# Reordering the start of a fused attention and mixture-of-experts kernel: early row writes ahead of late loads, the first tile's scaling on VectorE

## The chip, the cores and the metric

The kernel runs on 1 core of one Trainium2 chip, in one launch. The metric is device time in microseconds, as the median of the runs shown. A run's profile gives one execution, with its span from the first to the last instruction.

## The reference

Inputs `q`, `k`, `v` have the shape (8, 8, 576, 64): 8 batches, 8 heads, 576 tokens, 64 dimensions. The result has 8 × 576 = 4608 rows of 512.

```python
kv = np.einsum('bhsd,bhse->bhde', k, v)
out = np.einsum('bhsd,bhde->bhse', q, kv)
rms = np.sqrt(np.mean(out * out, axis=-1, keepdims=True) + 1e-06)
x = out / rms * g_norm          # then reshaped to 4608 rows of 512
logits = x @ w_gate             # 8 experts
e_idx = np.argmax(logits, axis=1)
gate_w = softmax(logits)[row, e_idx]
eom = 1 / (1 + np.exp(-(x @ w_output_gate)))
for e in range(8):              # rows whose best expert is e
    h = np.maximum(x[mask] @ w1[e], 0)      # 512 -> 1024
    out[mask] = gate_w * eom[:, e] * (h @ w2[e])   # 1024 -> 512
```

So each row goes to one expert out of eight, and which one is known only once its attention row is there.

## The kernel before, in words

**Tiles.** The 4608 tokens are 36 tiles of 128. For each of the 8 batches the kernel forms the `kv` matrix (`kv_part`, five steps of TensorE: four quarters of 128 tokens and a remainder of 64), transposes it (`kvT_part`, L589), multiplies it by the gate weights (`m_part`, L598), and then `out_tile` (L628) makes rows and logits of a tile of 128 tokens in one set of products, evicts them (`evict`, L677: rows to `xrow`, squares, logits), and writes pairs of tiles to the DRAM tensor `xs` (`xwrite`, L1050).

**Routing.** `route` (L711) runs in groups of 9, 7, 10 and 10 tiles on VectorE: the scale 1/rms of each row and head, logits, the best expert, the row's rank among its expert's rows (matmuls into `rps`), and a table of the rows of each expert (one-hot matrices `la` of VectorE, ScalarE and GpSimd, matmuls into `tblps`, L991). The table becomes row numbers in `gidx`. The scales go to small DRAM tensors (`xr0`, `xr`, `xt`).

**The early part.** The first 16 tiles (`EARLY`) are made and routed in `early` (L1108). After them the first two tiles of rows of every expert are known (the runs 0 to 7, 256 rows each). From then on the dense work goes on run by run (`run`, L1414), 8 runs of 256 rows and 8 of the rest, and what is left of the attention part (batches 4 to 7, tiles 16 to 35) is a generator, `late` (L1225), of which the dense loop takes one step, `next(rest)`, after each of its eight blocks of products.

**The first tile.** Run 0 is expert 0. The rows of its first 128 places are gathered from `xs` by an indirect DMA of GpSimd (`gather_row`, L315, called at L1006), their scales from `xr0` (L1200), both queued on GpSimd; `scale_rows` (L303, called at L1208) multiplies rows by scales on GpSimd (`scale_heads`, L298, is the multiplication on any engine). The second tile's gathers stand behind that on GpSimd (L1013), and its multiplication is on VectorE (L1491). `stage` (L322) transposes a tile on TensorE (L334, into `tps`); for run 0 ScalarE copies the result, times `g_norm`, to `xw` in fp32 (L338), then to the high part of a two-part form (`hi`, L340), and VectorE makes the low part `lo` (L341). `mm1_part` (L351) forms the first products of run 0 straight from `xw` and the unsplit weights `wraw`, for four of the eight blocks of 128 columns, first tile before second. All other products take three matmuls of high and low parts (`mm1`, L365, and `mm2`, L403).

**What sets the order.** Every engine's order is the program's order in this stretch (a manual schedule): TensorE, ScalarE, VectorE, GpSimd and SyncE each take their instructions as they are written. SyncE issues nearly all loads and the `xs` writes in one queue. `loads` is the list of early loads; `early_extra` holds those of batch 4 (four key-value quarters of 512 KB, one remainder) with query load 8 put third (L515 and L516); `send` issues the next of them, or a part of the first weights; `late_loads` holds all later ones. `constants(n)` puts n matmuls of constants into TensorE's order. The writes of tiles 14 and 15 (`held_row`, L668) are held back until all 16 tiles are done (L1183).

**Around L1183 to L1208**, in order: the held rows and the last write of `xs`; the rest of `early_extra`; the first step of `late` (quarters 0 and 1 of batch 4); the routing of the second group, with pauses numbered by `at_pause`: at 1 the second step of `late` (tile 16), at 6 the gather of the first tile's scales, the second quarter of the first weights (behind a GpSimd mark, `issue_mark`), two late loads and the third step (quarters 2 and 3), at 8 the scaling. `first_tile` (L1218) puts five constant matmuls, the fourth step (the remainder), `stage(0, 0)` and two constant matmuls. After the first products `stage(0, 1)` and two more steps of `late` follow (tile 17, `kvT_part`; L1501 to L1503), then `run(0)`.

```python
def scale_heads(x, tl, eng, heads=slice(0, H)):
    v = x.rearrange("p (h d) -> p h d", d=D)[:, heads]
    f = tl[:, heads].unsqueeze(2).to_broadcast(list(v.shape))
    return eng.tensor_tensor(out=v, in0=v, in1=f, op=ALU.mult)
```

Of the kernel before, what the change touches and what calls it, by code (L numbers as in the profile page):

```python
# [155 lines left out]
def body(ctx: ExitStack, tc: tile.TileContext, kvm, rem, qT, w1, w2, kc, xs, xr0, xr, xt, tab, out):  # L156
# [165 lines left out]
    def stage(i, k, eng=None):  # L322
# [13 lines left out]
        if not i:  # L336
            xw[k] = take([P, 4, P], F32, "xw")
            nc.scalar.activation(xw[k], ps, AF.Copy, scale=gcol[:, 0:1])  # L338
# [3 lines left out]
                                       in1=hi.bitcast(F32), op0=ALU.mult, op1=ALU.subtract)  # L342

# [172 lines left out]
    early_extra[2:2] = q_loads(nq + 1)  # L516
    late_loads = []
    g = EARLY
    for b in range(FIRST_B, B + 1):
        parts = []  # L520
        if b < B:
            kv = kv_loads(b) if b > FIRST_B else []
            parts = [kv[0:2], kv[2:4], rt_loads(b) if b > FIRST_B else []]
        for x, part in enumerate(parts):
            late_loads += part
            if (b > FIRST_B or x != 1) and g < tiles_ready(b - 1):
                late_loads += q_loads(g // 2 + 1)
                g += 1
        while g < tiles_ready(b - 1):
            late_loads += q_loads(g // 2 + 1)  # L530
            g += 1
# [21 lines left out]
    def kv_part(b):  # L553
# [6 lines left out]
        for s in range(5):  # L560
            if s in ((2, 4) if b >= FIRST_B else (1, 2, 3, 4)):
                yield
# [148 lines left out]
    def route(gi):  # L711
# [297 lines left out]
        else:  # L1009
# [6 lines left out]
            for _ in places(0, tacc[:, 0].rearrange("p (e t) -> p e t", t=TMAX), 0, TA):  # L1016
# [78 lines left out]

    def run_out(limit):
        nonlocal done_tiles
        if done_tiles < limit:
            out_tile(done_tiles)
# [8 lines left out]
    def early():  # L1108
# [50 lines left out]
        for k in range(4):  # L1159
# [3 lines left out]
            if k == 1:  # L1163
                run_out(lim)
                send(1)
                send(1)
# [18 lines left out]
        while early_extra:  # L1185
            send(1)
# [3 lines left out]
        while routing:  # L1190
# [4 lines left out]
            if k == 1:  # L1195
                next(rest)
            if k < 4:
                constants((2, 1, 2, 2)[k], tick[0])
            elif k == 6:
                first_tail = behind(gather_tail(0, 0, P, xr0), ranked[0])  # L1200
                behind(wload(0, 1, w1s.pop(0)), nc.gpsimd.memset(issue_mark, 1.0))
                assert len(xfree) > 1
                load([late_loads.pop(0) for _ in range(2)], xfree)
                next(rest)
            elif k == 7:
                constants(1, tick[0])
            elif k == 8:
                scale_rows(0, 0)  # L1208
# [9 lines left out]
    def first_tile():  # L1218

        constants(5)  # L1220
        next(rest)
        stage(0, 0)
        constants(2)

    def late():  # L1225
# [5 lines left out]
        for b in range(FIRST_B, B + 1):  # L1231
            lim = tiles_ready(b - 1)
            if b < B:
                kv = kv_part(b)
                for x in range(3):
# [3 lines left out]
                    if (b > FIRST_B or x != 1) and run_out(lim):  # L1239
# [4 lines left out]
                if run_out(lim):  # L1244
# [169 lines left out]
    def run(i, unit):  # L1414
# [4 lines left out]
        for f in range(8):  # L1419
# [5 lines left out]
            if i == 0 and f in (0, 2):  # L1425
# [59 lines left out]
    with tc.manual_schedule(engines=MAN):  # L1485
# [14 lines left out]
        load(late_loads, xfree, spare[0])  # L1500
        stage(0, 1)  # L1501
        next(rest)
        next(rest)  # L1503
# [122 lines left out]
```

## Time and profile before

| | us |
|---|---|
| median of 3 runs | 567.25 (565.82 to 567.77) |
| the profiled execution | 567.7 |
| its span, first to last instruction | 565.8 |
| TensorE busy in the span | 548.0 |
| VectorE, ScalarE, GpSimd busy | 346.7, 288.4, 220.6 |
| mean granted TensorE clock | 0.995 |

Times in the rows below are microseconds from the start of the span. PE is TensorE, PEld its weight loads, DVE VectorE, ACT ScalarE, POOL GpSimd and SP SyncE; a "q" behind a name is that engine's queue of waits and DMA issues. A name such as `xg<-xs,gix` reads "written, from what", L267 is line 267 of the kernel, and in brackets stands how long the engine was idle before and what ended that. Issues of DMAs are not their landings: a transfer is still on its way when its row ends.

### The profile page before, as it was taken

The page shows a single profiled execution, that of the slowest core. Times are in us where ns is not written, and L with a number is a line of the kernel's source. Part 1 is how long each engine was busy: PE and PEld are TensorE (multiplying, and loading weights), DVE is VectorE, ACT ScalarE, POOL GpSimd, SP SyncE. Part 2 cuts the span into 40 slices and gives each one's busy share as a digit, 9 for nine tenths or more (in the row PEclk, how much of TensorE's full clock was granted, in tenths as well). Part 3 has the DMA queues.
Part 4 walks back from the last instruction along what each step waited for, and adds up shares of the span by engine and source line. Part 5 has one row for each costly group of instructions (what it writes and reads, how often), then busy time and mean ns, then how long its engine had stood idle before and what let it go on. Part 6 is the DMA issues. An engine that isn't in the chain of part 4 may idle for free.

```text
span 565.8 us, 12002 instructions
## 1 busy us (share of the span) xinstructions
PE 548.0 (97%) x4602; PEld 473.0 (84%) x4602; DVE 346.7 (61%) x693; ACT 288.4 (51%) x546; POOL 220.6 (39%) x247
## 2 busy tenths in 40 slices
PE   8997899999999999999999999999999999999995
PEld 4784688988888889898989889898897978888884
DVE  2269567565798999785858556256363554647540
ACT  1464377575767567655644434345353554546330
POOL 4342446222323343342856225144252533644301
PEclk9999899999999999999999999999999999999999
DMA  8999799997857575677664256264565646466201
GB/s 332 409 409 403 266 394 378 409 409 253 302 187 262 176 273 178 231 233 236 225 223 151 105 165 195 92 195 137 166 202 156 191 141 178 159 196 192 78 5 39
DMA packets 38285, 126.33 MB, mean 223 GB/s; under 512 B 6525, under 2 KB 7790, under 8 KB 38225
## 3 DMA queue, kind: packets, MB, share of 16 engines
q1 hardware_dynamic: 29664, 105.26, 52.9%
q0 software_dynamic: 8416, 20.01, 10.9%
q8 instruction: 38, 0.62, 0.5%
q10 hardware_dynamic: 144, 0.25, 0.1%
q14 instruction: 23, 0.18, 0.1%
HBM read 106.01 MB, written 20.04 MB: 223 GB/s over the span
## 4 chain that ended last, share of the span: by engine, by line
PE 86%; DMA 6%; issue 2%; ACT 2%; DVE 1%; POOL 1%; SPq 0%; POOLq 0%
PE hps L388 37%; PE yps L424 35%; PE ops L654 5%; DMA ld<-kvm 5%; PE tps L334 3%; PE yps L418 3%; PE kvps L575 3%; DMA wraw<-w 1%; ACT xrow L663 1%; DMA out<-y,oidx 0%; PE cps L547 0%; DVE wlo L247 0%; ACT gp L685 0%; PE kvTps L593 0%; PE mps L605 0%
## 5 line engine op out<-in xcount | busy, mean ns | idle before, releaser
L388 PE MATMUL hps<-xT,whi 128*128 128x256 f32 (+8 forms) x992 | 212.8, 307 | 0.7 <-DVE hT L398 0.6
L424 PE MATMUL yps<-whi,hT 128*128 128x512 f32 (+3 forms) x592 | 199.5, 400 | 0.0
L388 PEld LDWEIGHTS hps<-xT,whi 128*128 128x128 f32 x992 | 164.2, 190 | 4.8 <-DVE hT L398 0.8
L388 PE MATMUL hps<-xT,wlo 128*128 128x256 f32 (+8 forms) x496 | 150.8, 304 | 0.0
L424 PEld LDWEIGHTS yps<-whi,hT 128*128 128x128 f32 (+3 forms) x592 | 110.1, 186 | 24.2
L424 PE MATMUL yps<-wlo,hT 128*128 128x512 f32 (+3 forms) x296 | 116.0, 392 | 0.0
L398 DVE SCALAR_TENSOR_TENSOR hT<-hps,hT 128x256 fp32r<-128x256 f32 (+9 forms) x168 | 63.3, 397 | 81.5 <-ACT hT L396 68.9
L437 POOL DMA_INDIRECT out<-y,oidx x42 | 43.6, 1039 | 174.1 <-ACT y L436 130.9
L235 DVE TENSOR_TENSOR wlo<-wraw,whi 128x1024 fp32r<-128x1024 f32 x66 | 81.6, 1238 | 48.0 <-ACT whi L232 46.8
L396 ACT ACTIVATE hT<-hps 128x256 fp32r<-128x256 f32 (+8 forms) x128 | 54.9, 429 | 97.4 <-PE hps L388 87.8
L388 PEld LDWEIGHTS hps<-xT,wlo 128*128 128x128 f32 x496 | 94.0, 190 | 0.3
L247 DVE TENSOR_TENSOR wlo<-wraw,whi 128x512 fp32r<-128x512 f32 x120 | 87.1, 726 | 3.5
L301 POOL TENSOR_TENSOR xg<-xg,tl 128x256 f32<-128x256 f32 (+9 forms) x81 | 59.2, 751 | 49.7 <-DMA tl<-xt,gidx 39.8
L246 ACT CAST whi<-wraw 128x512 fp32r<-128x512 f32 x120 | 73.5, 612 | 0.0
L232 ACT CAST whi<-wraw 128x1024 fp32r<-128x1024 f32 x66 | 69.4, 1051 | 0.0
L424 PEld LDWEIGHTS yps<-wlo,hT 128*128 128x128 f32 (+3 forms) x296 | 55.2, 187 | 10.2
L267 POOL DMA_INDIRECT xg<-xs,gidx x41 | 41.7, 1018 | 47.7 <-PE hps L388 32.9
L436 ACT ACTIVATE y<-yps,tl 128x512 f32<-128x512 f32 (+3 forms) x37 | 25.6, 691 | 59.5 <-PE yps L424 46.9
L267 POOL DMA_INDIRECT tl<-xt,gidx x41 | 45.1, 1101 | 25.3 <-PE hps L388 18.4
L340 ACT ACTIVATE xT<-tps,cf 128x512 fp32r<-128x512 f32 (+8 forms) x42 | 27.3, 650 | 49.9 <-PE tps L334 49.0
L341 DVE SCALAR_TENSOR_TENSOR xT<-tps,cf,xT 128x512 fp32r<-128x512 f32 (+8 forms) x42 | 29.4, 700 | 29.4 <-ACT xT L340 28.9
L654 PE MATMUL ops<-aug,ld 64*64 64x80 f32 (+1 forms) x960 | 32.4, 244 | 1.6 <-ACT gp L685 0.6
(183 smaller groups left out, 431.7 us busy)
## 6 DMA issues: line engine op xcount, KB each, us to landing
wraw<-w SPq DMA_DIRECT2D x128, 512.0 KB
ld<-kvm SPq DMA_DIRECT2D x32, 512.0 KB
ld<-qT SPq DMA_DIRECT2D x18, 512.0 KB
xs<-xrow SPq DMA_DIRECT2D x18, 512.0 KB
ld<-rem SPq DMA_DIRECT2D x4, 512.0 KB
out<-y,oidx POOLq DMA_INDIRECT x42
xg<-xs,gidx POOLq DMA_INDIRECT x41
tl<-xt,gidx POOLq DMA_INDIRECT x41
```

What stands on the lines that cost most here:

```text
L232: he.copy(hi, r)
L235: eng.tensor_tensor(out=lo, in0=r, in1=hi.bitcast(F32), op=ALU.subtract)
L246: nc.scalar.copy(hi[:, h], r[:, h])
L247: nc.vector.tensor_tensor(out=lo[:, h], in0=r[:, h], in1=hi.bitcast(F32)[:, h], op=ALU.subtract)
L267: return nc.gpsimd.indirect_dma_start(out=o[:M, :], out_offset=None, in_=dram[0:XE] if i < E else dram, in_offset=bass.IndirectOffsetOnAxi ...
L301: return eng.tensor_tensor(out=v, in0=v, in1=f, op=ALU.mult)
L388: seq.append(nc.tensor.matmul(ps[:, :C], w[:, o:o + P], x[d][:, :C], start=(d == 0 and k == 0), stop=(d == 3 and k == 2)))
L396: nc.scalar.activation(h[:, 0:C], ps[:, :C], AF.Relu)
L398: nc.vector.scalar_tensor_tensor(out=h[:, l:l + b - a], in0=ps[:, a:b], scalar=0.0, in1=h[:, a:b].bitcast(F32), op0=ALU.max, op1=ALU.subtract)
L424: seq.append(nc.tensor.matmul(ps[:M], a, b, start=(f == 0 and n == 0), stop=(f == 7 and n == 2)))
L437: i_ = nc.gpsimd.indirect_dma_start(out=out, out_offset=bass.IndirectOffsetOnAxis(ap=oidx[i // E][:M, RUNS[i][0], t:t + 1], axis=0), in_=y ...
L654: nc.tensor.matmul(ps[c0:c0 + step_, u, p * W:(p + 1) * W], qt[g // 2][r, p, q0:q0 + step_], augs[b % 3][r, p, :], start=True, stop=True)
```

## The change

It does this, and nothing else:

- `early_extra` no longer holds query load 8, which becomes the first of `late_loads`. The third quarter of batch 4 is issued behind the last `xs` write instead of ahead of it, the fourth quarter and the remainder at pause 1, behind the write of the second group's scales.
- Tile 16 is no longer made at pause 1 (four constant matmuls stand there instead of one) but after the first tile's first products, ahead of `stage(0, 1)`, with its eviction behind the next step. Tile 17 becomes the last step of batch 4, two steps later. Quarters 2 and 3 of batch 4 are a step each, the remainder goes behind `stage(0, 0)`, and the step at pause 1 is left out.
- The first tile's scaling goes from GpSimd to VectorE, between the first two parts of `places` in the second group's routing. The second tile's gathers no longer stand behind it on GpSimd.
- The second quarter of the first weights waits for the landing of the first tile's scales instead of GpSimd's mark. At pause 6 one query load and one key-value load follow it instead of two key-value loads; three constant matmuls are added.
- In run 0, ScalarE writes `xw` in two halves. `hi` and `lo` are made later, by `parts_of_rows`, from `xw` in SBUF instead of from PSUM.
- The splits of the third and fourth quarters of the first weights move from blocks 0 and 2 of run 0 to blocks 1 and 3.

```diff
@@ stage @@
-            nc.scalar.activation(xw[k], ps, AF.Copy, scale=gcol[:, 0:1])
+            for c in (0, 2):
+                nc.scalar.activation(xw[k][:, c:c + 2], ps[:, c:c + 2], AF.Copy, scale=gcol[:, 0:1])
+            return
...
+    def parts_of_rows(k):
+
+        hi, lo = (a[:, :, k * P:(k + 1) * P] for a in xT[0])
+        nc.scalar.copy(hi, xw[k])
+        nc.vector.tensor_tensor(out=lo, in0=xw[k], in1=hi.bitcast(F32), op=ALU.subtract)
@@ loads @@
-    early_extra[2:2] = q_loads(nq + 1)
...
-            if (b > FIRST_B or x != 1) and g < tiles_ready(b - 1):
+            if b > FIRST_B and g < tiles_ready(b - 1):
@@ kv_part @@
-            if s in ((2, 4) if b >= FIRST_B else (1, 2, 3, 4)):
+            if s in ((2, 4) if b > FIRST_B else (2, 3, 4) if b == FIRST_B else (1, 2, 3, 4)):
@@ route, second group @@
-            for _ in places(0, tacc[:, 0].rearrange("p (e t) -> p e t", t=TMAX), 0, TA):
+            todo = places(0, tacc[:, 0].rearrange("p (e t) -> p e t", t=TMAX), 0, TA)
+            next(todo)
+            scale_heads(xg[(0, 0)], tails[(0, 0)], vec)
+            for _ in todo:
@@ run_out @@
-            out_tile(done_tiles)
+            evict = out_tile(done_tiles, True)
+            if evicts is None:
+                evict()
+            else:
+                evicts.append(evict)
@@ early @@
             if k == 1:
                 run_out(lim)
-                send(1)
-                send(1)
...
         for r in rows:
             r()
-        while early_extra:
-            send(1)
+        send(1)
         next(rest)
...
             if k == 1:
-                next(rest)
+                send(1)
+                send(1)
+                assert not early_extra
             if k < 4:
-                constants((2, 1, 2, 2)[k], tick[0])
+                constants((2, 4, 2, 2)[k], tick[0])
             elif k == 6:
                 first_tail = behind(gather_tail(0, 0, P, xr0), ranked[0])
-                behind(wload(0, 1, w1s.pop(0)), nc.gpsimd.memset(issue_mark, 1.0))
-                assert len(xfree) > 1
-                load([late_loads.pop(0) for _ in range(2)], xfree)
+                behind(wload(0, 1, w1s.pop(0)), first_tail)
+                load([late_loads.pop(0)], free)
+                load([late_loads.pop(0)], xfree)
                 next(rest)
+                constants(3)
...
             elif k == 8:
-                scale_rows(0, 0)
                 constants(1, tick[0])
@@ first_tile @@
-        constants(5)
         next(rest)
+        constants(3)
         stage(0, 0)
-        constants(2)
+        next(rest)
+        parts_of_rows(0)
+        constants(1)
@@ late @@
-                for x in range(3):
+                for x in range(3 if b > FIRST_B else 4):
...
-                    if (b > FIRST_B or x != 1) and run_out(lim):
+                    if (b > FIRST_B or x == 3) and run_out(lim):
...
-                if run_out(lim):
+                if b > FIRST_B and run_out(lim):
@@ run @@
-            if i == 0 and f in (0, 2):
+            if i == 0 and f in (1, 3):
                 split(0, 1, f // 2 + 2)
@@ after early @@
+        evicts = []
+        next(rest)
         stage(0, 1)
         next(rest)
-        next(rest)
+        evicts.pop()()
+        evicts = None
+        parts_of_rows(1)
```

## Rows read from the trace of the kernel before

**Rows 1.** Busy time by stretch: us, per engine busy (instructions), clock, DMA share, GB/s
```profile
40.00:60.00 20.00, 15.90 (x339) 10.47 (x334) 16.86 (x58) 8.99 (x25) 6.28 (x8) 1.00 0.92 360
100.20:132.60 32.40, 32.40 (x427) 28.19 (x425) 19.38 (x33) 20.85 (x43) 8.26 (x10) 1.00 1.00 393
```

**Rows 2.** TensorE's waits from 66 us on: total us, times, longest
```profile
PE ops L654 <- ACT gp L685: 0.6, 1, 0.6
PE hps L388 <- DVE hT L398: 0.6, 1, 0.6
```

**Rows 3.** SyncE's queue in order of time: start us, us, what it issues
```profile
44.01 0.33 SPq L538 DMA_DIRECT2D ld<-qT  x1
45.22 0.33 SPq L538 DMA_DIRECT2D ld<-kvm  x1
46.51 2.77 SPq L1054 DMA_DIRECT2D xs<-xrow  x2
49.37 1.20 SPq L538 DMA_DIRECT2D ld<-kvm  x1
50.66 0.40 SPq L538 DMA_DIRECT2D ld<-rem  x1
52.28 0.33 SPq L752 DMA_DIRECT2D xr<-xtail  x1
```

**Rows 4.** The chain that ended last: start us, us, what
```profile
49.37 7.55 DMA ld<-kvm
...
56.96 0.69 PE kvps L575 x16
```

**Rows 5.** GpSimd in order of time, idle time and releaser in brackets
```profile
56.71 1.10 POOL L267 DMA_INDIRECT xg<-xs,gix  x1 [7.72 <-DMA xr<-xtail]
58.11 0.98 POOL L267 DMA_INDIRECT tl<-xr,gix  x1 [0.30 <-issue]
...
61.27 1.04 POOL L301 TENSOR_TENSOR xg<-xg,tl 128x512 f32<-128x512 f32 x1 [2.07 <-DMA tl<-xr,gix]
62.46 0.99 POOL L267 DMA_INDIRECT xg<-xs,gidx  x1
...
76.56 1.91 POOL L267 DMA_INDIRECT tl<-xr,gidx  x1 [2.92 <-PE hps L360]
```

**Rows 6.** VectorE in order of time
```profile
55.27 0.22 DVE L883 TENSOR_TENSOR rw<-rps,ohb 128x56 f32<-128x56 f32 x1 [0.46 <-PE rps L877]
...
57.19 0.74 DVE L913 TENSOR_SCALAR la<-ni,rlon 128x128 bf16<-128x128 f32 x3
59.64 0.17 DVE L1012 TENSOR_TENSOR gidx<-tacc,tblps 128x16 int32<-128x16 f32 x1 [1.71 <-PE tblps L991]
...
68.09 0.69 DVE L301 TENSOR_TENSOR xg<-xg,tl 128x512 f32<-128x512 f32 x1 [1.88 <-DMA tl<-xr,gidx]
...
76.40 1.23 DVE L235 TENSOR_TENSOR wlo<-wraw,whi 128x1024 fp32r<-128x1024 f32 x1 [0.51 <-ACT whi L232]
```

**Rows 7.** TensorE in order of time
```profile
62.37 1.12 PE L334 MATMUL tps<-ident,xg 128*128 128x128 f32 x4 [2.15 <-POOL xg L301]
...
64.27 4.49 PE L360 MATMUL hps<-xw,wraw 128*128 128x128 f32 x32
68.83 0.66 PE L334 MATMUL tps<-ident,xg 128*128 128x128 f32 x4
69.42 0.78 PE L654 MATMUL ops<-aug,ld 64*64 64x80 f32 x32
...
70.41 1.95 PE L360 MATMUL hps<-xw,wraw 128*128 128x128 f32 x16
...
73.75 2.54 PE L360 MATMUL hps<-xw,wraw 128*128 128x128 f32 x16
```

**Rows 8.** Busy time by stretch, columns as in rows 1
```profile
56.00:58.00 2.00, 1.04 (x18) 0.76 (x19) 1.86 (x8) 1.50 (x4) 1.10 (x1) 1.00 0.48 184
62.00:64.00 2.00, 1.63 (x6) 1.00 (x6) 1.28 (x6) 0.47 (x1) 1.55 (x3) 0.56 0.94 313
```

More of the change, by code (lines that the diff above doesn't have):

```diff
@@ L1500, in body @@
         load(late_loads, xfree, spare[0])
+        evicts = []
+        next(rest)
         stage(0, 1)
         next(rest)
-        next(rest)
+        evicts.pop()()
+        evicts = None
+        parts_of_rows(1)
         for i in range(E - 1):
```

## The prediction

> **What bounds the kernel now.** I read four views in turn. The first is the busy time by stretch [rows 1]: between 100.20 and 132.60 us TensorE is busy for 32.40 of 32.40 us, between 40 and 60 us for only 15.90 of 20. The second is TensorE's waits from 66 us to the end [rows 2]: two waits of 0.6 us each. So from about 66 us on the time is TensorE's own work, and a change that removes no work can gain only by starting that work earlier, or by putting work into idle time. The third view is the time line of each engine around the start, and there one chain stands out. SyncE issues the last early `xs` writes behind a query load at 44.01 and a key-value load at 45.22 [rows 3]; GpSimd sits idle for 7.72 us until it can gather the first tile at 56.71 and its scales at 58.11, multiplies rows by scales from 61.27 for 1.04 us, and only then gathers the second tile at 62.46 [rows 5]. TensorE transposes the first tile at 62.37 after an idle 2.15 us and starts its products at 64.27 [rows 7]. The fourth is the clock: 56 to 58 us had 1.00, but 62 to 64 us had 0.56 granted [rows 8], the lower of the two levels (1.2 and 2.4 GHz) for most of that stretch, right behind the idle 2.15 us.
>
> **The sum is made against the profiled execution**, 567.7 us with a span of 565.8; the median of the runs shown is 567.25, 0.45 lower, and I take the difference worked out here off the median.
>
> **The change, part by part.**
>
> 1. *SyncE's order.* The query load and the third key-value quarter leave the place ahead of the two `xs` writes. Is the queue really what the gather waits for? The second write goes out at about 49.0 to 49.3 (the row of two ends at 49.28) and the gather starts 7.4 later; the key-value load issued right behind it needs 7.55 [rows 3, 4]. Both wait as long, so it is a queue. Its pace is the spacing of issues, 44.01, 45.22, 46.51 [rows 3]: 1.25 us for 512 KB. Two loads fewer in front: 2.5 us, gather at 54.2. The writes themselves can't go earlier, since ScalarE's copies set their issue.
>
> 2. *Scales.* They are issued 1.40 behind the rows (58.11 − 56.71), so at 55.6; their other condition, the ranking matmul, is over by 55.27 [rows 5, 6]. From their issue to the multiplication took 3.16 us: 58.8. If the loads now running behind the writes slow them as the second tile's gathers were slowed (62.46 to 68.09 is 5.63, 56.71 to 61.27 is 4.56 [rows 5, 6]), 59.8.
>
> 3. *VectorE multiplies.* It takes 0.69 us there for 1.04 on GpSimd [rows 5, 6], but VectorE is in order, and the table add at 59.64 with two short instructions (0.17 each by the first's row) now stands ahead: 60.2 if that add comes no earlier. It followed an idle 1.71, and the last `la` row ends at 57.93 [rows 6]. With one key-value batch moved behind the table's matmuls (0.69 [rows 4]) it could come as early as 58.4, so scaling starts between 58.9 and 60.2. I take 59.9, near the late end, since I can't name all of the 1.71. Scaled at 60.6, transposes at 60.65 for 62.37: **−1.7** (−1.4 to −2.7).
>
> 4. *Transposes to products* took 1.90 at the low clock [rows 7, 8]. Now come the transposes at 0.66 (the second tile's row), a key-value batch at 0.69 and one constant matmul, while ScalarE copies in halves: 1.4 to 1.9, I take 1.6, **−0.3**.
>
> 5. *Clock.* The 32 products took 4.49 us, the 16 at 70.41 1.95 [rows 7], so 3.9 for 32 at the full clock. TensorE's idle time before the transposes should shrink to about 1 us, so I take **−0.6** (0 if the clock falls all the same). The products end at 66.15 for 68.76, 2.6 earlier.
>
> 6. *The moved tiles.* The first of them ran ahead of the first tile, in a stretch with idle time [rows 1], and now stands in the busy stretch: **+0.8** (0.78, the row at 69.42 [rows 7]). The second was already in the busy stretch and is only moved on; each key-value batch taken out of there comes back one step later. The moved tile covers the second tile's scaling: its gather follows the table add at 59.8 instead of 62.46, since GpSimd no longer multiplies first, so its rows are scaled at 66.2 for 68.78, ahead of 66.9, when the products and the moved tile are done. The second transposes: 66.9 for 68.83 [rows 7], **−1.9** (−0.7 with the low clock and the late table, −2.9 with the early table).
>
> 7. *Behind that point.* The splits of the first weights move one step, so the second 16 products should not take 2.54 but 1.95 [rows 7]: up to −0.6. Against it, ScalarE has the moved tile's eviction and the copy of `hi` from SBUF ahead of the first ReLU, and the second moved tile needs a PSUM pair that ScalarE frees: up to +0.7. I take 0 for both. The smaller gathers, the dropped mark on GpSimd and the wait of SyncE's next weights for the scales' landing (58.8 to 59.8, where it was the mark behind the scales' issue, 58.11 + 0.98 = 59.1) cost nothing: nobody is waiting behind them but loads with time to spare, and if those were late the rival on the load stream is what happens.
>
> Sum: 567.7 − 1.9 = 565.8 in the profiled execution's terms, **565.3** off the median. About 0.3%, 1.7 us, is what a measurement of this kernel tells from no change.
>
> **A rule weighed.** GpSimd's scales gather at 76.56 took 1.91 us, 0.93 more than the one at 58.11, while VectorE ran a subtraction with two inputs at 76.40, whose 1.23 is not visibly lengthened [rows 5, 6]. The change brings such a pair together: VectorE's scaling at 59.9 and the second tile's gather at 59.8. By the row the gather loses 0.93, its rows are ready at 67.1 instead of 66.2, 0.2 behind the moved tile: 565.5. The Trainium skill, "SBUF — State Buffer", section "Who interferes with whom", says that a VectorE instruction with two SBUF inputs and a GpSimd instruction that reads SBUF share a read interface, and that whichever starts second waits for the whole of the first. The row agrees that there is a conflict, but not on who loses; if here it is VectorE, that is the second rival.
>
> **Rivals.**
>
> - *The early end of step 3* (0.15): table add at 58.4. Total −2.9: 564.3. For it: nothing in the rows fills the 1.71. Against: the idle is named as a wait for the table's matmul, which stays.
> - *The scaling waits for the gather* (0.14): GpSimd starts the second tile's gather at 59.8 and holds VectorE's scaling, due at 59.9, until it ends 0.98 later [rows 5]. The first tile is 0.9 later, net −1.0: 566.3. Against: no VectorE row here is seen to lose by a gather.
> - *The write isn't queue-bound* (0.13), so the change doesn't do what it says: GpSimd's row names the small `xr` write as its releaser [rows 5], which SyncE issues at 52.28. Then the first tile gains 0.35 (0.69 for 1.04) and 0.3 from the halves, and pays 0.8: no change, 567.2. Against: the equal waits of step 1.
> - *The load stream becomes the bound, slower* (0.12). DMA is at 1.00 from 100.20 on [rows 1]. The last quarter of the sixth batch (b = 5) was the 8th load from the second quarter of the first weights and is now the 11th, as the query load and two second weights come ahead: 3 × 1.25 = 3.75 us later, while TensorE comes 1.9 earlier, though one step later in its order. If the stream as a whole comes no sooner, TensorE stands there for up to 3.75: 567.25 − 1.9 + 3.75 = 569.1. It decides from a stall of 3.6 us on. Against: DMA was half idle at 56 to 58 us (0.48 [rows 8]), and the third weights' load, which waits for the second tile's gathers, goes out some 2.5 earlier, so most of the 3.75 comes back.
>
> **How the numbers follow.** The forecast has 0.46 (564.5 to 566.1 by step 3 and the clock; about three quarters of it lie under 565.55), the rivals 0.15, 0.14, 0.13 and 0.12 in that order. Faster by over 0.3%: 0.46 × 0.75 + 0.15 + a little of the third = 0.53; within: the rest of these and the fourth, 0.35; slower: 0.12. The range leaves out the ends of the first rival and most of the last: 563.6 to 567.7.
>
> **What would show it.** In the changed profile: GpSimd's first gather near 54.2 (step 1), VectorE's first scaling near 59.9 (3), transposes near 60.7 and products at most 1.7 later (4), a granted clock of 1.00 throughout 60 to 68 us (5), the second transposes near 66.9 behind the moved tile (6), no wait of TensorE over 0.6 after that (7). I am wrong if the first gather stays at 56.7, if the table add is still what VectorE waits for and goes later than 59.64, or if TensorE waits for a key-value load behind 70 us.

## The result and the profile after

| | before | changed |
|---|---|---|
| median of 12 runs, us | 568.49 (565.82 to 569.68) | 571.30 (569.42 to 573.16) |
| ratio, 95% interval | | 1.0054 (1.0034 to 1.0075) |
| the profiled execution, its span | 567.7, 565.8 | 570.05, 568.2 |
| TensorE busy in the span | 548.0 | 548.9 |
| mean granted TensorE clock | 0.995 | 0.998 |

Slower by 0.5%, 2.8 us, where 2 less were forecast: 565.3, off the 567.25 of the three runs shown until then; twelve runs of the kernel before have 568.49. The first fence is the time line of the changed kernel, one engine after another: start, duration, engine and line, what; in brackets the idle time before and what ended it.

```profile
54.09 1.10 POOL L267 DMA_INDIRECT xg<-xs,gix  x1 [5.61 <-DMA ld<-kvm]
...
59.40 0.94 POOL L267 DMA_INDIRECT tl<-xr,gidx  x1 [0.30 <-issue]
...
57.71 0.17 DVE L1019 TENSOR_TENSOR gidx<-tacc,tblps 128x16 int32<-128x16 f32 x1 [0.30 <-PE tblps L998]
59.51 0.69 DVE L301 TENSOR_TENSOR xg<-xg,tl 128x512 f32<-128x512 f32 x1 [1.16 <-DMA tl<-xr,gix]
...
66.52 0.69 DVE L301 TENSOR_TENSOR xg<-xg,tl 128x512 f32<-128x512 f32 x1 [2.01 <-DMA tl<-xr,gidx]
...
59.48 0.33 SPq L222 DMA_DIRECT2D wraw<-w  x1
59.90 0.38 SPq L545 DMA_DIRECT2D ld<-qT  x1
...
60.26 0.66 PE L334 MATMUL tps<-ident,xg 128*128 128x128 f32 x4 [1.22 <-DVE xg L301]
...
61.95 3.81 PE L368 MATMUL hps<-xw,wraw 128*128 128x128 f32 x32
67.32 0.78 PE L661 MATMUL ops<-aug,ld 64*64 64x80 f32 x32 [1.56 <-DMA ld<-qT]
68.03 0.65 PE L334 MATMUL tps<-ident,xg 128*128 128x128 f32 x4
...
69.25 2.05 PE L368 MATMUL hps<-xw,wraw 128*128 128x128 f32 x16 [0.35 <-ACT xw L339]
...
72.48 0.78 PE L661 MATMUL ops<-aug,ld 64*64 64x80 f32 x32 [0.82 <-issue]
73.19 2.05 PE L368 MATMUL hps<-xw,wraw 128*128 128x128 f32 x16
...
77.59 0.49 PE L661 MATMUL ops<-aug,ld 64*64 64x80 f32 x11 [0.38 <-issue]
78.02 0.51 PE L396 MATMUL hps<-xT,whi 128*128 128x256 f32 x2
...
79.64 1.33 PE L582 MATMUL kvps<-ld 128*64 128x64 f32 x32
```

Read against [rows 5 to 7], everything up to the first products came as forecast: the gather at 54.09 for 56.71, the products' end at 65.76 for 68.76, 3.0 us ahead. Then the lead melts. TensorE stands 1.56 us at the moved tile for a query load, and the second transposes are 0.8 ahead (68.03 for 68.83). Before the next products it is 0.56 ahead (73.19 for 73.75). At block 4, the first line of L396, it is level with before, and a half of a key-value batch that the kernel before has done by then (L582, the last line) is still to come. The kernel before at that place:

```profile
76.93 1.15 PE L575 MATMUL kvps<-ld 128*64 128x64 f32 x32
78.01 0.51 PE L388 MATMUL hps<-xT,whi 128*128 128x256 f32 x2
```

The second view is TensorE's waits from 64 to 400 us (total, times, longest), to set against the two waits of [rows 2].

```profile
PE ops L661 <- DMA ld<-qT: 1.9, 2, 1.6
...
PE hps L396 <- DVE hT L406: 1.1, 3, 0.6
```

The key-value half (1.33), a second query wait (0.39, at 87.56) and 0.5 more for `hT` make 2.2 of the 2.4 us by which the span grew.

One execution doesn't tell all. Of the changed kernel's 20 executions (12 here, 8 in a later run) 10 had a mean clock of at least 0.994 and took 570.6 us on average; 10 had at most 0.993 and took 572.9. The profiled one is of the first kind. The mean is a coarse sign: the kernel before has 0.995 in the execution whose clock fell to 0.56 for a while [rows 8], and run 11 has 0.994 in one in which it fell too.

### The profile page after: what moved, and what is told of

Same layout as the page of the kernel before. It is cut to its first block, busy times and chain, and to the rows that moved or that the text cites. A ratio compares the mean times of both kernels' runs of the same rounds, so it can differ in the third digit from the quotient of the medians.

```text
span 568.2 us, 12012 instructions
## 1 busy us (share of the span) xinstructions
PE 548.9 (97%) x4605; PEld 473.2 (83%) x4605; DVE 347.3 (61%) x694; ACT 288.5 (51%) x548; POOL 223.7 (39%) x245
## 4 chain that ended last, share of the span: by engine, by line
PE 83%; DMA 9%; issue 2%; ACT 2%; SPq 1%; DVE 1%; POOL 0%; POOLq 0%
PE hps L396 35%; PE yps L432 35%; DMA ld<-kvm 5%; PE ops L661 4%; PE tps L334 3%; PE yps L426 3%; PE kvps L582 2%; DMA ld<-qT 2%; DMA xs<-xrow 1%; DMA tl<-xr,gix 1%; SPq L545 1%; ACT xrow L670 1%; DMA out<-y,oidx 0%; PE kvTps L600 0%; PE mps L612 0%
## 5 line engine op out<-in xcount | busy, mean ns | idle before, releaser
L396 PE MATMUL hps<-xT,whi 128*128 128x256 f32 (+8 forms) x992 | 212.9, 307 | 1.2 <-DVE hT L406 1.1
L396 PEld LDWEIGHTS hps<-xT,whi 128*128 128x128 f32 x992 | 164.2, 189 | 5.7 <-DVE hT L406 1.7
L396 PE MATMUL hps<-xT,wlo 128*128 128x256 f32 (+8 forms) x496 | 150.8, 304 | 0.0
L235 DVE TENSOR_TENSOR wlo<-wraw,whi 128x1024 fp32r<-128x1024 f32 x66 | 83.1, 1262 | 46.4 <-ACT whi L232 45.8
L396 PEld LDWEIGHTS hps<-xT,wlo 128*128 128x128 f32 x496 | 94.0, 189 | 0.3
L247 DVE TENSOR_TENSOR wlo<-wraw,whi 128x512 fp32r<-128x512 f32 x120 | 85.4, 712 | 3.6
L301 POOL TENSOR_TENSOR xg<-xg,tl 128x256 f32<-128x256 f32 (+8 forms) x80 | 61.6, 791 | 47.4 <-DMA tl<-xt,gidx 38.9
L267 POOL DMA_INDIRECT xg<-xs,gidx x41 | 43.3, 1056 | 48.0 <-PE hps L396 31.5
L342 ACT ACTIVATE xT<-tps,cf 128x512 fp32r<-128x512 f32 (+8 forms) x40 | 25.9, 649 | 50.4 <-PE tps L334 49.6
L343 DVE SCALAR_TENSOR_TENSOR xT<-tps,cf,xT 128x512 fp32r<-128x512 f32 (+8 forms) x40 | 27.9, 697 | 28.6 <-ACT xT L342 28.2
```

The lines of the kernel that those rows point to most:

```text
L235: eng.tensor_tensor(out=lo, in0=r, in1=hi.bitcast(F32), op=ALU.subtract)
L247: nc.vector.tensor_tensor(out=lo[:, h], in0=r[:, h], in1=hi.bitcast(F32)[:, h], op=ALU.subtract)
L267: return nc.gpsimd.indirect_dma_start(out=o[:M, :], out_offset=None, in_=dram[0:XE] if i < E else dram, in_offset=bass.IndirectOffsetOnAxi ...
L396: seq.append(nc.tensor.matmul(ps[:, :C], w[:, o:o + P], x[d][:, :C], start=(d == 0 and k == 0), stop=(d == 3 and k == 2)))
```

## The experiments

Each run stands beside runs of the kernel before on the same chip: 568.32 us for the first four, 568.52, 568.54 and 568.43 for the later groups.

**1. Query load 8 ahead of the weights' wait.** In the fence above SyncE issues the moved tile's query load at 59.90, right behind the weights that wait for the scales' landing (59.48).

```diff
+                load([late_loads.pop(0)], free)
                 behind(wload(0, 1, w1s.pop(0)), first_tail)
-                load([late_loads.pop(0)], free)
```

> Edit to the changed kernel: query load 8 is issued ahead of the second quarter of the first weights, so it no longer stands on SyncE behind the landing of the first tile's scales. Theory L (the late query load gives the start back): tile 16 follows the products without its wait of 1.56 us, the second transposes come at about 66.5 instead of 68.03, and the time falls by 1.5, from 571.3 to about 569.8. Rival R (the second tile's scales, which landed at 66.49, are as late): tile 16 stands at 65.8, but the transposes come at 67.2 at the earliest, 0.8 sooner: 570.5. Rival P (the PSUM pair and ScalarE's evictions behind the transposes give back whatever comes sooner): the products of block 4 start at 78.0 as in the changed kernel, 571.3. In all three the first scales may land up to 1.25 later, because one more load of 512 KB is ahead of them; that would be taken off.

573.29 us, 1.0092 (1.0069 to 1.0116). TensorE no longer waits for the load, but the scales, now behind it, land later. VectorE's time line:

```profile
62.06 0.69 DVE L301 TENSOR_TENSOR xg<-xg,tl 128x512 f32<-128x512 f32 x1 [3.62 <-DMA tl<-xr,gix]
```

2.5 us later than 59.51. TensorE is idle 2.86 us ahead of the transposes, and the 32 products take 6.04. No execution of six had a clock above 0.993.

**2. The mark on GpSimd again.** The weights wait for GpSimd's mark, as before the change.

```diff
-                behind(wload(0, 1, w1s.pop(0)), first_tail)
+                behind(wload(0, 1, w1s.pop(0)), nc.gpsimd.memset(issue_mark, 1.0))
```

> Edit to the changed kernel: the second quarter of the first weights waits for a GpSimd mark behind the issue of the first scales (as in the kernel before) instead of for their landing. SyncE then goes on at about 56.6 instead of 59.48. Theory L: query load 8 lands before 65.8, the wait of 1.56 is gone, and the whole load stream comes 2 to 3 us sooner, so the waits for loads behind it are gone too: 571.3 - 1.5 to 571.3 - 2.0, about 569.5. Rival C (the wait kept the loads away from the scales' gather): the first scales land later than 59.43, by up to 2.5 (two loads of 1.25), VectorE's scaling goes from 59.5 to 61 or 62, and the time is 571 to 572. Rival P: no change, 571.3.

572.63 us, 1.0081 (1.0052 to 1.0110). Again the query wait is gone, the scaling later (61.25) and the products at 6.14: the wait is bought off with the thing it protected.

**3. Tile 16 early, with the first edit.**

```diff
         next(rest)
-        constants(3)
+        run_out(EARLY + 1)
         stage(0, 0)
```

> Edit to the changed kernel: query load 8 as in the run before last, and tile 16 is made ahead of the first transposes, in place of three constant matmuls; tile 17 takes tile 16's place behind the first products, and each later step of the attention part comes one block sooner. Theory L, with the moved tile as the second loss: tile 16 goes into the idle 1.22 us ahead of the first transposes (58.2 to 59.0, if the query load has landed by then), so 0.8 us less is left for the busy stretch: 1.5 + 0.8 = 2.3 sooner, 569.0. With rival R 0.8 + 0.8: 569.7. Rival K (the key-value loads of batch 5 are as late as before and are now wanted a block sooner): TensorE waits for them between 72 and 80 us, up to 2 us, 571. Rival Q: the query load lands after 59 and the first transposes wait for tile 16; then the first products start later than 61.95 by as much.

573.08 us, 1.0092 (1.0078 to 1.0106). The tile stands 2.10 us for the query load there too, and all five executions had a clock of 0.991 or less.

**4. Tile 17 in its old place,** a step earlier.

```diff
-                if b > FIRST_B and run_out(lim):
+                if run_out(lim):
                     more()
```

> Edit to the changed kernel: only tile 17 stands ahead of the products that write the same PSUM pair for the gate columns of batch 4, instead of behind them; nothing of the loads is touched. Theory P (turn-around of the one pair between those products, ScalarE's copy and tile 17): TensorE's 0.82 us ahead of tile 17 falls to 0.2 or less: 571.3 - 0.6 = 570.7. Theory L: 0.82 goes, but a like wait comes back ahead of the gate products or of tile 18 in the next block, since the pair has to turn around as often; 571.1 to 571.3. The wait of 1.56 for the query load stays in both.

574.71 us, 1.0109 (1.0083 to 1.0134). VectorE's scaling, TensorE's time line, then its waits from 64 to 300 us:

```profile
61.03 0.69 DVE L301 TENSOR_TENSOR xg<-xg,tl 128x512 f32<-128x512 f32 x1 [2.76 <-DMA tl<-xr,gix]
...
58.86 0.69 PE L582 MATMUL kvps<-ld 128*64 128x64 f32 x16 [1.28 <-DMA ld<-kvm]
...
64.59 6.24 PE L368 MATMUL hps<-xw,wraw 128*128 128x128 f32 x32
```

```profile
PE mps L612 <- ACT gp L692: 2.5, 1, 2.5
```

The 0.82 of tile 17 is replaced by 2.5: the gate products that follow its rows now wait for ScalarE. So nothing speaks against moving tile 17 on. Up to 60 us this kernel is the changed one, instruction by instruction; yet its key-value quarter came late, and its scaling at 61.03 for 59.51. So the landing of the scales itself varies from execution to execution, and here the clock fell. The stretches (us, busy time of PE, PEld, DVE, ACT and POOL, then the clock, the DMA share and GB/s) show it:

```profile
60.00:62.00 2.00, 1.16 (x4) 0.26 (x3) 0.93 (x4) 0.00 (x0) 0.37 (x2) 0.50 0.44 129
...
66.00:68.00 2.00, 2.00 (x11) 2.00 (x11) 1.90 (x10) 0.00 (x0) 0.00 (x0) 0.50 1.01 373
```

0.50 is the lower level, 1.2 GHz. Four edits, none faster; in each of the four profiles the products take 5.23 us or more, for 3.81. So the clock became the theory to test.

**5 and 6. Idle time filled, and laid bare.** Both leave the changed kernel's order and vary only the constant matmuls of `first_tile`: nine for three, or none.

```diff
+        constants(4)
         next(rest)
-        constants(3)
+        constants(5)
         stage(0, 0)
```

> Edit to the changed kernel: 4 constant matmuls ahead of the fourth key-value quarter and 5 behind it, where 3 stood behind it; TensorE then has no long idle time before the first transposes, whether that quarter and the first scales land early or late. Theory C (the clock decides: in some executions of the changed kernel it falls to the lower level just before the first transposes, and the products then take about twice as long): the granted clock is 1.00 from 50 to 72 us, the mean clock of every execution is at least 0.994, and the time is that of the changed kernel's profiled execution, 570.05, plus up to 0.5 because the constants end at about 60.7 (57.6 + 4 x 0.27 + 0.69 + 5 x 0.27) and the rows are ready at 60.2: 570.0 to 570.6. Rival N (the spread of the changed kernel comes from the landing of its loads, the clock only goes with it): 571.3 and the same spread of 3.7 us.

```diff
         next(rest)
-        constants(3)
         stage(0, 0)
```

> Edit to the changed kernel: the 3 constant matmuls ahead of the first transposes are left out and nothing else. Theory C: TensorE's idle time there grows from 1.22 to 2.0 us or more, the clock falls in nearly every execution, and the time is about 2.8 above an execution that keeps its clock: 572.8 to 573.3, with a mean clock of 0.992 or less. Rival N: 0.8 us of work that nobody waits for is gone; 571.3.

Filled: 570.53 us, 1.0028 (1.0008 to 1.0048), 11 of 12 executions at a clock of 0.994 or more. Bare: 572.85, 1.0068 (1.0051 to 1.0084), all six at 0.992 or less. The changed kernel beside them, run 8 below, took 572.64. TensorE's time line, filled and then bare:

```profile
60.95 0.66 PE L334 MATMUL tps<-ident,xg 128*128 128x128 f32 x4
...
62.65 4.14 PE L368 MATMUL hps<-xw,wraw 128*128 128x128 f32 x32
67.70 0.78 PE L661 MATMUL ops<-aug,ld 64*64 64x80 f32 x32 [0.91 <-DMA ld<-qT]
...
81.30 0.69 PE L582 MATMUL kvps<-ld 128*64 128x64 f32 x16 [0.57 <-DMA ld<-kvm]
```

```profile
60.91 1.12 PE L334 MATMUL tps<-ident,xg 128*128 128x128 f32 x4 [2.01 <-DVE xg L301]
...
63.72 5.43 PE L368 MATMUL hps<-xw,wraw 128*128 128x128 f32 x32
```

And the bare kernel by stretch, columns as above:

```profile
60.00:62.00 2.00, 1.09 (x6) 0.77 (x6) 1.74 (x6) 0.00 (x0) 1.06 (x2) 0.57 0.77 221
...
66.00:68.00 2.00, 2.00 (x15) 2.00 (x15) 0.10 (x1) 0.00 (x0) 0.00 (x0) 0.72 0.99 362
```

Both transpose at the same moment, 60.9. Behind an idle 2.01 us the clock is at the lower level from about 60 to 67 us; behind constant matmuls it stays at 1.00, and the products end 2.4 us earlier (66.79 for 69.15). In medians the fill takes 2.1 off the changed kernel as it ran beside it (run 8, 572.64), but only 0.8 off the first twelve executions (571.30). The query wait stays in the filled kernel (0.91), and so does a gap to before of 2.0.

**7. The loads and tiles in their old places,** filled as in run 5. What stays of the change is the third and fourth key-value quarters behind the `xs` writes, the scaling on VectorE, the halves, the later splits, and the wait of the weights.

```diff
+    early_extra[2:2] = q_loads(nq + 1)
@@ early @@
             if k == 1:
                 run_out(lim)
+                send(1)
@@ pause 1 @@
                 assert not early_extra
+                next(rest)
             if k < 4:
-                constants((2, 4, 2, 2)[k], tick[0])
+                constants((2, 1, 2, 2)[k], tick[0])
@@ pause 6 @@
-                load([late_loads.pop(0)], free)
-                load([late_loads.pop(0)], xfree)
+                load([late_loads.pop(0) for _ in range(2)], xfree)
@@ late @@
-                    if (b > FIRST_B or x == 3) and run_out(lim):
+                    if (b > FIRST_B or x in (0, 3)) and run_out(lim):
@@ after early @@
-        evicts = []
-        next(rest)
         stage(0, 1)
         next(rest)
-        evicts.pop()()
-        evicts = None
+        next(rest)
```

> Edit to the changed kernel: query load 8 is issued early again (one load of 512 KB ahead of the last writes), tile 16 is made at pause 1 and tile 17 behind the second transposes as in the kernel before, and the constants are those of the run before last but one (4 and 5). What is left of the change is the third quarter behind the writes, the scaling on VectorE, the copies in halves and the later splits. Theory C with theory L: the first gather comes at 55.4 (54.1 + 1.25), the first products at about 63.3 and end at 67.1 with the full clock, nothing waits for query load 8, the second transposes come at 67.2 to 67.5 where the kernel before has 68.83, and the 0.8 us for the moved tile isn't paid: 1.3 to 1.6 below the kernel before, 566.8 to 567.1. Rival R (the second tile's scales, with loads in the way, set the second transposes): they come at 68.5 or later, 568.1 to 568.4, as the kernel before.

568.77 us, 1.0000 (0.9986 to 1.0014): all of the loss is gone, and nothing is won. GpSimd's time line, TensorE's, and ScalarE's in this kernel and (L663) in the kernel before:

```profile
55.47 1.10 POOL L267 DMA_INDIRECT xg<-xs,gix  x1 [6.92 <-DMA xs<-xrow]
```

```profile
72.55 2.05 PE L368 MATMUL hps<-xw,wraw 128*128 128x128 f32 x16
74.53 0.78 PE L662 MATMUL ops<-aug,ld 64*64 64x80 f32 x32
75.24 1.32 PE L583 MATMUL kvps<-ld 128*64 128x64 f32 x22
...
77.71 0.36 PE L583 MATMUL kvps<-ld 128*64 128x64 f32 x5 [0.37 <-issue]
78.00 0.50 PE L396 MATMUL hps<-xT,whi 128*128 128x256 f32 x2
```

```profile
77.76 0.59 ACT L671 COPY xrow<-ops 128x512 f32<-128x512 f32 x1 [3.64 <-remote]
...
77.31 0.59 ACT L663 COPY xrow<-ops 128x512 f32<-128x512 f32 x1 [0.94 <-PE ops L654]
```

One 512 KB load ahead of the writes makes the gather 1.38 us later (55.47 for 54.09): the queue is real. TensorE is 1.2 us ahead at 72.55 (73.75 before) and starts block 4 at 78.00, where before had 78.01. The lead goes between 74 and 78 us, in small stalls among the key-value products that the profile can't name. ScalarE shows it too: it stands idle for 3.64 us ahead of the eviction of tile 18, which starts at 77.76, although by their row that tile's products (74.53) are over at 75.31. Before, the eviction came at 77.31, so it isn't earlier either.

**8. The changed kernel again,** beside runs 5 to 7, with no edit.

> The changed kernel itself, once more, on the chip of these runs. Theory C: its executions fall into two groups, near 570.0 with a mean clock of 0.994 or more and near 572.8 with 0.992 or less, and the median lies between, 570.5 to 572.8. Rival N: no relation between the mean clock and the time.

572.64 us, 1.0066 (1.0043 to 1.0088), two of eight executions at a clock of 0.994 or more. That it is 1.3 above the first 571.30 goes with the shares: eight of the first twelve were at 0.994 or more. Its profiled execution (571.16, span 569.3) is a second profile of the changed kernel. TensorE's time line, then its waits from 64 us on:

```profile
66.43 0.78 PE L661 MATMUL ops<-aug,ld 64*64 64x80 f32 x32
...
77.11 0.50 PE L396 MATMUL hps<-xT,whi 128*128 128x256 f32 x2
```

```profile
PE hps L396 <- DVE hT L406: 1.4, 2, 0.8
...
PE tps L334 <- POOL xg L301: 1.2, 1, 1.2
```

The clock was at 1.00 from 56 to 72 us and the moved tile didn't wait for its query load; TensorE is 0.9 ahead of the kernel before at block 4. Still the span is 3.5 longer: the key-value half, 0.50 for a key-value load at 79.92, and, behind 200 us, the two waits shown, where the kernel before has one of 0.6 for `hT` [rows 2]. So the clock and the moved tile's wait don't explain every execution.

**9. The key-value step one block later,** on top of run 7, in case its loads are what is waited for.

```diff
                         yield
+                    if b == FIRST_B + 1 and x == 0:
+                        yield
```

> Edit to the kernel with the tiles back (568.77, the kernel before 568.52 beside it): quarters 2 and 3 of batch 5, and every step behind them, come one block of products later. In that kernel TensorE was 1.2 us ahead of the kernel before until 72.55 and had lost all of it by 78.00, in those two quarters (2.8 us for 1.15). Theory S (the load stream sets this point: an earlier start of TensorE is worth nothing unless what it needs at 76 us comes earlier too): with the block in between the quarters run at 1.15 and the 1.2 stay: 567.5, which is below the kernel before by 1.0. Rival M (whatever TensorE runs between 75 and 78 us loses 1.2 there, loads or not): the products of block 4 take that time instead, 568.7.

568.48 us, 1.0005 (0.9991 to 1.0020). TensorE's time line, then ScalarE's:

```profile
79.12 0.50 PE L396 MATMUL hps<-xT,whi 128*128 128x256 f32 x2 [1.36 <-DVE hT L406]
```

```profile
77.03 0.59 ACT L671 COPY xrow<-ops 128x512 f32<-128x512 f32 x1 [3.66 <-PE hps L396]
```

Block 4 now runs ahead of the step, from 74.49, and block 5 starts at 79.12 behind a wait of 1.36 for `hT`. That `hT` is late because ScalarE, which works ahead of it, stands idle for 3.66 us at the eviction of tile 18, as in run 7. TensorE was 1.96 ahead at 71.79 (73.75 before); with the same work done, 0.5 is left (81.46 for 81.97), and in the median nothing.

**10. Run 7 with GpSimd's mark,** the edit of run 2.

> Edit to the kernel with the tiles back: the second quarter of the first weights waits for a GpSimd mark behind the issue of the first scales, not for their landing, so that the load stream goes on some 2 us sooner (about 58.0 for 60.20). Theory S: quarters 2 and 3 of batch 5 run without the loss at 76 us, but the first scales land 1 to 2 us later as in the run that did this to the changed kernel (61.2 for 59.4), so that the first products end at about 67.5 to 68.5 instead of 66.7: 568.0 to 568.5 against the kernel before at 568.5. Rival C (what the first tile loses goes through to the end): 569.5 to 570. Rival M: 568.8.

568.61 us, 1.0004 (0.9990 to 1.0017): no difference.

**11. Run 5 with query load 8 early,** the tiles where the change puts them.

```diff
+    early_extra[2:2] = q_loads(nq + 1)
...
                 run_out(lim)
+                send(1)
...
-                load([late_loads.pop(0)], free)
```

> Edit to the changed kernel with its constants filled (570.53): query load 8 is issued early as in the kernel before, ahead of the last writes; tiles 16 and 17 stay where the change put them. Theory L (the query load is what the moved tile loses by): the 0.9 us wait for it is gone, 569.6. Theory T (the moved tiles themselves: 0.8 us of work in the busy stretch, then 0.35 for ScalarE's copy, 0.8 and 0.4 behind the turn-around of the pair and in tile 18): the query load only covered the landing of the second tile's scales at 67.60, and the time stays near 570.5; then most of the 1.8 us between this and the kernel with the tiles back (568.77) is the tiles' place.

568.92 us, 1.0004 (0.9993 to 1.0015): 1.6 less than run 5. Its profiled execution, at 570.52 the slowest of the twelve, is one in which the clock fell all the same. TensorE's time line:

```profile
63.55 5.44 PE L368 MATMUL hps<-xw,wraw 128*128 128x128 f32 x32
68.91 0.78 PE L662 MATMUL ops<-aug,ld 64*64 64x80 f32 x32
```

The moved tile doesn't wait. So the place of query load 8 is the second part of the loss; the moved tiles cost 0.15 beside run 7, less than can be measured.

**12. The kernel before, filled.**

```diff
         next(rest)
+        constants(7)
         stage(0, 0)
```

> Edit to the kernel before: 7 constant matmuls ahead of the first transposes, in the idle 2.15 us in which its clock fell to 0.56. Theory C: the clock stays at 1.00 and the first products end about 1 us sooner, but the second transposes wait for the second tile's rows at 68.78 all the same, so the time stays at 568.5 (568.2 to 568.6): in the kernel before the fall of the clock was covered, in the changed kernel it isn't. Rival: the clock cost the kernel before as well, 567.5.

567.92 us, 0.9985 (0.9974 to 0.9997): the fastest of all, 0.6 below the kernel before. TensorE's time line:

```profile
62.39 0.66 PE L334 MATMUL tps<-ident,xg 128*128 128x128 f32 x4 [0.57 <-POOL xg L301]
...
63.82 3.84 PE L360 MATMUL hps<-xw,wraw 128*128 128x128 f32 x32 [0.35 <-ACT xw L338]
68.44 0.65 PE L334 MATMUL tps<-ident,xg 128*128 128x128 f32 x4 [0.78 <-DVE xg L301]
...
77.61 0.50 PE L388 MATMUL hps<-xT,whi 128*128 128x256 f32 x2
```

The products end at 67.66 for 68.76, 1.1 earlier, but 0.78 us of waiting for the second tile's rows takes their place: before, those rows (scaled by 68.78 [rows 6]) were ready just as the slow products ended. 0.4 is left at block 4. Since the fill gains on the kernel before as well, the filled run 7 should be set beside this one: it is 0.85 slower, so what stays of the change there wins nothing and may cost a little.

**13. Run 7 without two loads:** quarters 2 and 3 of batch 5 aren't loaded, and the first two serve again.

```diff
-            parts = [kv[0:2], kv[2:4], ...
+            parts = [kv[0:2], kv[2:4] if b != FIRST_B + 1 else [], ...
```

> Edit to the kernel with the tiles back (568.77): the loads of quarters 2 and 3 of batch 5 are left out, and the products of these quarters read quarters 0 and 1 once more, so the key-value matrix of batch 5 is not the reference's; TensorE's work is the same. Theory S (the load stream sets what TensorE can do between 74 and 79 us): 1 MB less ahead of everything that follows, the quarters run at 1.15 and the 1.2 us gained at the start stay, 567.5 or less. Rival M (what is lost between 74 and 79 us hangs on no load of TensorE's): 568.6 to 568.8 again, with the quarters still at 2 us or more, or the same loss in the work next to them.

567.85 us, 0.9995 (0.9985 to 1.0005). TensorE's time line:

```profile
77.12 0.45 PE L584 MATMUL kvps<-ld 128*64 128x64 f32 x7 [0.40 <-issue]
77.50 0.51 PE L396 MATMUL hps<-xT,whi 128*128 128x256 f32 x2
```

The stalls stay (three, of 0.28 to 0.40 us), though these operands have long been there: it isn't their loads. Block 4 starts 0.5 earlier than in run 7, but the span ends only 0.1 earlier (565.7 for 565.8).

**14 and 15. VectorE's scaling alone in the kernel before,** and that with the constants of run 12.

```diff
+            next(todo)
+            scale_heads(xg[(0, 0)], tails[(0, 0)], vec)
...
-                scale_rows(0, 0)
```

> Edit to the kernel before, one part of the change alone: the first tile is scaled on VectorE between the first two parts of the places, and GpSimd's scaling is left out. The first rows are ready 0.35 sooner (0.69 for 1.04), GpSimd gathers the second tile at about 59.9 instead of 62.46, so that its rows are scaled 1 to 2 us sooner than 68.78. If the clock falls as in the kernel before (idle 1.8 for 2.15), the first products end at 68.4 and the second transposes come there, 0.4 sooner: 568.1 against 568.5. Rival M: 568.5.

> The same with 7 constant matmuls ahead of the first transposes, as in the run that filled the kernel before (567.92). The clock stays at 1.00, the first products end near 67.3, and the second tile's rows are ready by then: the second transposes come at 67.3 to 67.6 where the filled kernel before has 68.44, and the time is 0.6 to 0.9 lower than its, 567.0 to 567.3. Rival M, or theory S: what TensorE gains is gone by 79 us, 567.9.

568.08 us, 0.9992 (0.9983 to 1.0001), and 568.06, 0.9989 (0.9976 to 1.0002). Both start block 4 earlier than 78.01 (77.59 and 77.42), and both spans end at 566.0, 0.2 later than that of the kernel before. In run 15 TensorE waits for `hT` three times behind 200 us, 1.3 us in all, where the kernel before waits 0.6 [rows 2]: its lead of 0.6 goes there.

## Why the prediction was wrong

**Steps 1 to 4 held.** The gather came at 54.09 (54.2 forecast), the scaling at 59.51 (59.9), the transposes at 60.26 (60.65), the products 1.69 later (1.6). The table add came earlier than my early bound, 57.71 for 58.4, but then the landing of the scales ended VectorE's wait, so the first rival's gain went unused. The scales took 4.0 us from issue to scaling, inside the bounds of step 2 for this execution; run 4, whose program is the same up to there, shows that they can land 1.5 us later, beyond these bounds.

**Step 5 failed in its bound.** In the profiled execution the forecast held (3.81 for 3.9). But "0 if the clock falls all the same" took the 4.49 of [rows 7] for the worst. In the changed order the products took 5.23 to 6.24 in each profile in which the clock fell (runs 1 to 4, 6 and 11), and in run 6 it stayed down to about 67 us, in run 4 all through 66 to 68. The kernel before had 1.00 again by then:

```profile
66.00:68.00 2.00, 2.00 (x20) 2.00 (x19) 0.17 (x2) 0.00 (x0) 0.00 (x0) 1.00 0.75 218
```

The kernel before pays little for its fall, since the second tile's rows end no earlier: filling it wins 0.6 (run 12). In the changed kernel a fill wins 2.1 (runs 5 and 8; 0.8 beside the first twelve executions). Runs 5, 6 and 8 differ in constant matmuls alone, so this part of the loss is the clock's.

**Step 6 failed in its cover.** "The moved tile covers the second tile's scaling" and "nobody is waiting behind them but loads with time to spare" contradict each other: query load 8 feeds the moved tile and is queued right behind that wait. TensorE stood 1.56 us for it in the profiled execution; in medians putting it back gained 1.6 (runs 5 and 11). How this comes about is shown in part: run 5's profile has 0.91 at the moved tile and 0.57 for a key-value load, run 11's has neither, but its TensorE runs 1.2 later there; and in run 8's profile the tile didn't wait. I looked at the queue that the load left, not at the one that it joined. The second tile's rows, forecast for 66.2, were scaled at 67.21, so the transposes could not have come at 66.9 in any case, and half of the 1.56 would have been spent without the query load; their scales, issued at 59.40, kept VectorE waiting until 66.52.

**Step 7, put at 0,** had a gain of 0.4 (2.05 and 2.05 for 1.95 and 2.54) and waits of 0.35, 0.82 (for ScalarE, as run 5's profile names it) and 0.38. Its premise, that what is won at the start stays won, fell in run 7: 1.2 us ahead at 72.55, level at 78.00, 568.77 in the median. Moving the key-value step (run 9) saves at most 0.5 of the lead there and nothing in the median; it isn't the mark (10) or the loads (13). In all four of these profiles ScalarE stands idle for 3.6 to 3.7 us ahead of tile 18's eviction, where the kernel before has 0.94. What holds that eviction, and TensorE beside it, is open. Further leads go behind 200 us, in waits for `hT` (run 15).

**The rivals.** *Slower* was right in sign. Its place, a key-value load behind 70 us, was worth 0.57 us in run 5; its real places were the query load and the clock. That the writes aren't queue-bound fell (54.09, 55.47). *The scaling waits for the gather*: GpSimd's gather runs from 59.40 to 60.34 and VectorE's scaling from 59.51 to 60.20; by themselves they take 0.98 and 0.69 [rows 5, 6], so neither waited. The Trainium skill, "SBUF — State Buffer", section "Who interferes with whom", has a VectorE instruction with two SBUF inputs block only a GpSimd instruction that reads SBUF, and infers that making the descriptors of a transfer needs the write side, which this one leaves free. The pair agrees with that; the gathers of 1.91 [rows 5] and 1.88 us (76.80 in the changed kernel), each beside a subtraction of 128x1024, don't.

**The sum by runs,** in medians: changed 572.64 (run 8), filled 570.53, the query load back 568.92, the tiles and loads back 568.77, before 568.52. Of the 4.1 us, 2.1 are the clock and 1.6 the query load's place; the rest is less than can be measured, and nothing of the 3.0 us won at the start arrives. With 571.30 for the changed kernel the loss is 2.8, and the clock's share 0.8. The query load was not put back without the fill, so the shares hold in this order only.

## What to carry to other kernels

When a transfer is moved, read the queue that it joins: what stands just ahead of it there, and who uses it first. When idle time ahead of light work shrinks but doesn't vanish, take the products behind it at the lower clock as one whole case, priced where nothing covers it, and try a few constant matmuls in the gap before anything else; in this kernel that was the only edit that beat the kernel before, by 0.6 us. And follow a lead from landmark to landmark before it is put into the sum: 3 us ahead at one point was none 12 us later. Take a second profile of the same kernel, too: this one's two profiles lose their time in different places.

## What was not expected of the hardware

- Executions of the same program had a mean clock of at least 0.994 in 10 cases of 20 and less in 10, which goes with 2.3 us of mean time. It is no strict relation: one execution at 0.999 took 572.74. Both profiled ones kept 1.00 around the first products; that it fell there in the others is inferred from the mean.
- The landing of the same scales spread by 1.5 us between executions: the first scaling came at 59.51 in the changed kernel and 61.03 in run 4, whose programs are alike until then.
- A gather of 64 bytes for each of 128 rows, issued at 59.40, kept its reader waiting until 66.52, 7.1 us, with seven loads issued behind it from 59.48 to 62.63.
